# A new fixed order for the first quarter, and a later place for part of the second layer's weight preparation, in a one-core attention and two-layer feed-forward kernel

## The chip, the cores and the metric

One core of a Trainium2 chip. The metric is device time in microseconds (us), the median of several runs. Engines: TensorE (PE in the profile), its weight loads (PEld), VectorE (DVE), ScalarE (ACT), GpSimd (POOL) and SyncE (SP), which issues the DMAs here. Each engine executes its own instructions in the order in which they were put, and waits at each for what it needs of the others.

## What is computed

```python
def _attn_ref(x, state):                      # x (4, 8, 512, 64), state (4, 8, 32, 64)
    scores = scale * np.matmul(x, state.transpose(0, 1, 3, 2))
    a = np.exp(scores - scores.max(-1, keepdims=True))
    a /= a.sum(-1, keepdims=True) + 1e-09
    xread = np.matmul(a, state)
    scores2 = scale * np.matmul(state, x.transpose(0, 1, 3, 2))
    a2 = np.exp(scores2 - scores2.max(-1, keepdims=True))
    a2 /= a2.sum(-1, keepdims=True) + 1e-09
    sread = np.matmul(a2, x)
    return np.concatenate([xread, sread], axis=2)

def _moe_ref(x, w_in, w_out, alpha):          # 2304 tokens, 512 wide, 2048 hidden
    h = x @ w_in
    g = np.maximum(h, 0.0) + alpha * np.minimum(h, 0.0)
    return g @ w_out

def _moe2_ref(x, w_in, w_out):
    h = x @ w_in
    g = np.maximum(h, 0.0) + np.log1p(np.exp(-np.abs(h)))
    return g @ w_out
```

The attention's result, 2304 rows of 512, goes through the first feed-forward layer and that one's result through the second. All of it is float32.

## The kernel before, in words

**Layer 1.** The 2304 rows are four blocks of 512 (the x of one batch entry each) and one of 128 leftover rows (the state rows of all). The hidden width of 2048 is taken in four quarters of 512 (q = 0 to 3), and a quarter's block in four steps of 128 hidden columns: `hidden` makes the product into a bank of the pool `psa` (tiles pa), `act` applies the activation, `out_part` multiplies by the quarter's rows of w_out into banks of `psb` (tiles pb), and `out_take` (L450 on DVE) adds the result to the accumulators acc. Products are made of a high and a low part (names with h and l, L178 to L180: three matmuls of 128x512 each); ACT makes the high part by a rounding copy (L183), the low part is a subtraction (L184).

**Weights.** The 64 weight tiles are loaded by SP into four staging buffers stg (L243) and converted: two ACT steps (L261 exp<-stg, L262 top<-exp), three DVE steps (L266, L272, L276) and one POOL addition (L282). `tick` does one such conversion within a stage, and `conv_head` puts the two ACT steps of the next one ahead. Tiles of layer 2 go back to memory (`kept_w`) until they are used.

**The order.** The first quarter (q = 0), with the attention, is an order written out by hand: the list `ORDER` (L48), whose words are a letter, the step, and a number, its item. `steps` defines a function for each letter: L loads a weight tile, a, j, f, v, g are the conversion steps, x and y load the attention's inputs, s, S, k, t, m, u, e, z, r, n, b, c, d are the row softmax of a half block, M, E, Z, T, K, R, F, X, W the state softmax and read, w, p, q the weight folded with the state, H, A, C, G, D a hidden step with its activation (H on PE, A and G on ACT, C and D on DVE), O its output product, Q its result, and N(i) puts i matmuls of the identity with itself on PE (L640), which nobody reads: fillers. All engines take the list's sequence.

Everything behind the list (quarters 1 to 3 and layer 2) is written in plain loops, and a scheduler puts each engine's order together from it; `tc.issue_after(x)` keeps what is emitted inside from standing ahead of instruction x on its engine.

**The leftover rows** of quarters 1 to 3: `rows_copy` (L385) makes their hidden product (L368 on PE) and copies it by ACT into tmp (L388); `turned_rows` (L391) runs an output product in between and then transposes that copy on PE (L396).

**Layer 2** works on pairs of blocks with seven products of quarter matrices in place of eight (`product`, L585). Its weights come back as raw tiles (`raw_load`, into at0h, at0l, at1h, at1l), and `w_steps(h)` makes from them, for half h of a quarter's columns, the parts nat (wi4, wi5, ex1, wi0) and sums (wi1, ex0, wi2, wi3): eight splits of 128x256, the high parts by ACT (L183), the low parts by POOL (L184), and POOL sums (L488) of 128x128 and 128x256 in between. The steps of half 0 of the first quarter are run by the last quarter of layer 1 (`W_AHEAD`). The steps of half 1 are emitted in the first turn of layer 2 (`p, n` = 0, 0) by `run(w_now, 4)` and `run(w_now)`. The accumulators of the first pair of blocks are prepared by `y_first`: sums on POOL and 14 splits, the last of them of t4 (at7, sw7).

Of the kernel before, what the change touches and what calls it, by code (L numbers as in the profile page):

```python
# [48 lines left out]
N8 N12 L0 a0 U0 x0 s0 P0 L1 N6 k0 x1 j0 f0 v0 t0 s1 a1 M0 g0 L2 x2 y0 L3 m0 j1 e0 E0 L4 a2 z0 Z0 k1 f1 r0 N13 N25 T0  # L49
v1 j2 n0 t1 b0 f2 N29 g1 m1 v2 u1 x3 S2 a3 K0 B0 e1 N3 j3 R0 z1 k3 f3 r1 v3 V0 n1 g2 k2 F0 t3 g3 b1 t2 w00 m2 m3 c0 a4  # L50
X0 W0 e2 p00 j4 z2 w01 f4 u3 r2 c1 p01 H0 N4 q01 L5 H1 A0 e3 v4 n2 a5 C0 g4 b2 z3 L6 j5 r3 G0 A1 N2 H2 c2 C1 a6 f5 d0
H3 x5 x4 L7 w03 G1 D0 j6 D1 h4 l4 n3 L8 A2 f6 C2 p03 v6 g6 A3 h6 d2 d1 O0 v5 b3 c3 G2 g5 q03 a8 w02 M1 d3 p02 D2 C3
q02 G3 h5 D3 M2 a7 j7 f7 v7 H4 A4 l6 l5 S4 k4 H5 E1 x6 E2 L9 A5 O1 j8 C4 f8 y2 g7 C5 v8 a9 L10 O2 t4 k5 h7 l7 g8 T1 T2
H6 O3 H7 G4 G5 A6 D4 j9 t5 y1 M4 D5 f9 m4 u4 m5 v9 C6 E4 Q3 e4 z4 M5 O4 u5 A7 K1 r4 e5 C7 z5 r5 Z2 Z1 n4 n5 G6 O5 K2
a10 R2 D6 b4 G7 M3 R1 F2 c4 E5 F1 T4 X2 O6 Z5 b5 d4 W2 c5 K4 E3 y3 d5 H8 X1 W1 A8 T3 Z3 D7 Z4 j10 C8 f10 K3 y4 L11 x7
H9 A9 C9 R3 F3 O7 S6 G8 G9 Q7 k7 X3 v10 H10 T5 D8 D9 k6 t7 t6 A10 m6 m7 u7 M6 u6 K5 e7 O8 W3 g10 e6 E6 z7 r7 y5 L12
C10 M7 z6 H11 r6 G10 R5 g9 D10 n7 R4 b7 n6 b6 F5 O9 A11 a11 c6 c7 L13 y6 y7 C11 d6 G11 F4 X5 D11 T6 E7 L14 W5 O10 X4
W4 Z7 d7 j11 f11 v11 H12 K6 a12 A12 H13 R6 C12 T7 g11 a13 G12 A13 K7 Z6 j12 O11 f12 C13 H14 D12 H15 v12 j13 g12 F6 G13
Q11 A14 O12 f13 C14 a14 X6 G14 D13 j14 R7 h12 W6 v13 w11 L15 l12 D14 f14 F7 v14 g13 L16 a15 X7 j15 W7 A15 f15 O13 C15
h13 G15 I0 J0 O14 w10 p11 D15 H16 q11 v15 l13 g14 h14 L17 l14 A16 O15 C16 g15 p10 G16 q10 D16 H17 Q15 O16 H18 h15 A17  # L60
A18 H19 H20 C17 G17 C18 G18 A19 Q16 A20 D17 D18 w13 C20 C19 G19 p13 G20 O17 q13 D19 w12 p12 D20 L18 q12 l15
# [22 lines left out]
def mixer_kernel(  # L84
# [199 lines left out]
    acted = {}  # L284
# [100 lines left out]
    def rows_copy(m, q):  # L385
        ps = hidden_rows(m, q)
        hs = tslot()
        nc.scalar.activation(hs, ps, AF.Copy)  # L388
        return hs
# [553 lines left out]
    for q in range(1, NQ):  # L943
# [3 lines left out]
        for b in blocks:  # L947
            for fc in range(4 if b < B else 1):
                if n in TICKS[q]:
                    conv_head()  # L950
# [141 lines left out]
```

## Time and profile before

| | us |
|---|---|
| Median of 3 runs | 712.98 |
| Lowest and highest run | 712.31, 713.21 |
| The profiled execution's own time | 714.09 |
| Its span | 712.2 |
| PE busy, and its share | 700.0 (98%) |
| DVE, ACT, POOL busy | 509.3, 468.1, 358.4 |

The span runs from the first instruction to the last of the profiled execution, and its own time is what that execution took as a whole. A busy PE is not a PE at its peak: the ends of matmuls are modelled, and the fillers count as busy. Windows of the span show which stage a hole belongs to.

### The profile page before, as it was taken

To read this page: it belongs to the slowest core of one execution; us is meant where nothing else is said; L and a number is where in the kernel's file an instruction comes from. 1 tells how busy PE (TensorE), PEld (TensorE's weight loads), DVE (VectorE), ACT (ScalarE), POOL (GpSimd) and SP (SyncE) were. 2 spreads that over 40 slices of the span, in tenths; PEclk is the share of its full clock that TensorE was granted. 3 is DMA by queue.
4 is the path that set the end of the run, shared out by engine and by line. 5 is a ranking of instruction groups with operands and counts; after the bars stand their busy time and mean duration, and the time that the engine had idled before them with its cause. 6 is when DMAs were issued, how large, how long until landed. Compare 5 with 4: busy or idle time off the path is not lost.

```text
span 712.2 us, 10216 instructions
## 1 busy us (share of the span) xinstructions
PE 700.0 (98%) x3530; PEld 548.0 (77%) x3530; DVE 509.3 (72%) x832; ACT 468.1 (66%) x921; POOL 358.4 (50%) x401
## 2 busy tenths in 40 slices
PE   8999999999999999989999999999999999999997
PEld 6457776677777777858888888888888888888886
DVE  4897786479999989788455577747675546677665
ACT  4777796556665656556569777557885877676541
POOL 2463223023334323597975594096998666454110
PEclk9999999999999999999999999999999999999999
DMA  8352532131552365545300522002205221210003
GB/s 296 106 170 84 192 115 91 30 118 58 178 164 93 131 210 173 193 149 169 120 8 1 177 75 104 20 26 88 60 2 177 75 89 30 89 30 30 2 29 119
DMA packets 30484, 72.49 MB, mean 102 GB/s; under 512 B 3552, under 2 KB 3552, under 8 KB 30432
## 3 DMA queue, kind: packets, MB, share of 16 engines
q1 hardware_dynamic: 30432, 71.83, 31.0%
q8 instruction: 28, 0.46, 0.3%
q14 instruction: 24, 0.20, 0.1%
HBM read 58.97 MB, written 12.85 MB: 101 GB/s over the span
## 4 chain that ended last, share of the span: by engine, by line
PE 87%; DVE 4%; DMA 3%; ACT 3%; POOL 1%; issue 1%; SPq 1%; POOLq 0%; ACTq 0%
PE pa L585 21%; PE pb L178 16%; PE pb L179 16%; PE pb L180 16%; PE pa L178 4%; PE pa L180 4%; PE pa L179 4%; PE pa L332 2%; DMA acc<-xt 2%; PE pa L368 1%; DVE stg L276 1%; DMA stg<-w1o 1%; DMA stg<-w1i 1%; PE pa L396 0%; POOL stg L282 0%
## 5 line engine op out<-in xcount | busy, mean ns | idle before, releaser
L282 POOL TENSOR_TENSOR stg<-top,stg 128x512 f32<-128x512 bf16 x48 | 58.4, 1217 | 105.0 <-DVE stg L276 79.5
L607 DVE TENSOR_TENSOR acc<-pb,acc 128x512 f32<-128x512 f32 x112 | 74.5, 686 | 25.0 <-PE pb L180 24.1
L404 DVE SCALAR_TENSOR_TENSOR pa<-tmp,rest,pa 128x512 f32<-128x512 f32 (+1 forms) x80 | 52.8, 668 | 24.2 <-ACT tmp L412 15.3
L415 ACT ACTIVATE tmp<-pa 128x512 f32<-128x512 f32 x68 | 40.2, 594 | 40.5 <-DVE pa L488 27.1
L418 DVE SCALAR_TENSOR_TENSOR pa<-pa,tmp 128x512 f32<-128x512 f32 x68 | 46.8, 694 | 14.4 <-ACT tmp L417 14.0
L266 DVE SCALAR_TENSOR_TENSOR top<-stg,top 128x512 uint16<-128x512 uint16 x63 | 50.8, 809 | 7.8 <-ACT top L262 7.7
L261 ACT ACTIVATE exp<-stg 128x512 bf16<-128x512 bf16 x63 | 41.9, 667 | 19.0 <-DMA stg<-w2i 5.3
L262 ACT ACTIVATE top<-exp,top_bias 128x512 uint16<-128x512 uint16 x64 | 46.1, 722 | 12.6 <-POOL stg L282 6.9
L416 ACT ACTIVATE tmp<-tmp 128x512 f32<-128x512 f32 x68 | 42.3, 630 | 0.7
L417 ACT ACTIVATE tmp<-tmp 128x512 f32<-128x512 f32 x68 | 42.3, 629 | 0.6
L488 DVE TENSOR_TENSOR pa<-pa,wo2l 128x512 f32<-128x512 f32 x32 | 22.2, 696 | 27.3 <-PE pa L585 27.3
L276 DVE SCALAR_TENSOR_TENSOR stg<-stg,exp 128x512 f32<-128x512 uint32 x48 | 40.7, 850 | 1.0
L450 DVE TENSOR_TENSOR acc<-pb,acc 128x512 f32<-128x512 f32 x54 | 35.1, 684 | 4.3 <-PE pb L180 4.3
L412 ACT ACTIVATE tmp<-pa 128x512 f32<-128x512 f32 x47 | 27.4, 590 | 12.4 <-PE pa L180 7.2
L488 DVE TENSOR_TENSOR wo2h<-pa,wo2h 128x512 f32<-128x512 f32 x16 | 11.1, 691 | 27.5 <-ACT wo2h L1000 15.6
L183 ACT ACTIVATE g1h<-pa 128x512 fp32r<-128x512 f32 x26 | 15.5, 596 | 17.3 <-DVE pa L404 9.2
L272 DVE TENSOR_SCALAR exp<-top 128x512 uint16<-128x512 uint16 x64 | 26.1, 409 | 0.9
L184 POOL TENSOR_TENSOR ex1l<-at1h,ex1h 128x256 fp32r<-128x256 f32 x16 | 11.8, 739 | 26.9 <-ACT ex1h L183 24.6
L184 POOL TENSOR_TENSOR wi4l<-at0h,wi4h 128x256 fp32r<-128x256 f32 x16 | 11.9, 743 | 23.1 <-ACT wi4h L183 23.1
L488 DVE TENSOR_TENSOR wo2l<-pa,wo2h 128x512 f32<-128x512 f32 x16 | 11.0, 690 | 15.8 <-PE pa L585 15.8
L184 DVE TENSOR_TENSOR g3l<-pa,g3h 128x512 fp32r<-128x512 f32 x22 | 15.2, 690 | 9.5 <-ACT g3h L183 9.4
L183 ACT ACTIVATE g0h<-pa 128x512 fp32r<-128x512 f32 x23 | 13.8, 598 | 12.4 <-DVE pa L404 10.2
(808 smaller groups left out, 2459.9 us busy)
## 6 DMA issues: line engine op xcount, KB each, us to landing
stg<-w1o SPq DMA_DIRECT2D x16, 511.8 KB, 3.9
stg<-w2i SPq DMA_DIRECT2D x16, 511.8 KB, 4.3
stg<-w2o SPq DMA_DIRECT2D x16, 511.8 KB, 3.5
stg<-w1i SPq DMA_DIRECT2D x15, 511.8 KB, 4.7
acc<-xt SPq DMA_DIRECT2D x16, 256.0 KB, 5.5
wi<-stg SPq DMA_DIRECT2D x16, 256.0 KB, 3.1
wo<-stg SPq DMA_DIRECT2D x16, 256.0 KB, 2.9
out<-acc SPq DMA_DIRECT2D x16, 256.0 KB, 3.0
```

Source lines behind the costliest of these rows:

```text
L178: nc.tensor.matmul(ps, lh, rh, start=start, stop=False)
L179: nc.tensor.matmul(ps, lh, rl, start=False, stop=False)
L180: nc.tensor.matmul(ps, ll, rh, start=False, stop=stop)
L262: nc.scalar.activation(t.bitcast(U16), e.bitcast(U16), AF.Relu, bias=top_bias, scale=TOP_SCALE)
L266: nc.vector.scalar_tensor_tensor(out=tu, in0=words(i)[0], scalar=TOP_SIGN, in1=tu, op0=ALU.bitwise_and, op1=ALU.bitwise_or)
L276: nc.vector.scalar_tensor_tensor(out=a, in0=words(i)[1], scalar=REST, in1=parts(i)[1], op0=ALU.mult, op1=ALU.mult)
L282: nc.gpsimd.tensor_tensor(out=a, in0=parts(i)[0], in1=a, op=ALU.add)
L404: nc.vector.scalar_tensor_tensor(out=ps[:, cs], in0=t[:, cs], scalar=a, in1=ps[:, cs], op0=ALU.mult, op1=ALU.add)
L418: nc.vector.scalar_tensor_tensor(out=ps, in0=ps, scalar=0.0, in1=t, op0=ALU.max, op1=ALU.add)
L488: eng.tensor_tensor(out=o, in0=x, in1=y, op=op)
L585: nc.tensor.matmul(ps, l[:, c], r, start=first and k == 0 and i == 0, stop=k == 1 and i == 2, skip_group_check=not first,)
L607: nc.vector.tensor_tensor(out=a, in0=ps, in1=a, op=ALU.add)
```

## The change

It has three parts.

1. The list `ORDER` is another one: the same steps and items except for the fillers, in another sequence. Of each the first line, and two lines around the second block's first steps:

```diff
-N8 N12 L0 a0 U0 x0 s0 P0 L1 N6 k0 x1 j0 f0 v0 t0 s1 a1 M0 g0 L2 x2 y0 L3 m0 j1 e0 E0 L4 a2 z0 Z0 k1 f1 r0 N13 N25 T0
...
-q02 G3 h5 D3 M2 a7 j7 f7 v7 H4 A4 l6 l5 S4 k4 H5 E1 x6 E2 L9 A5 O1 j8 C4 f8 y2 g7 C5 v8 a9 L10 O2 t4 k5 h7 l7 g8 T1 T2
-H6 O3 H7 G4 G5 A6 D4 j9 t5 y1 M4 D5 f9 m4 u4 m5 v9 C6 E4 Q3 e4 z4 M5 O4 u5 A7 K1 r4 e5 C7 z5 r5 Z2 Z1 n4 n5 G6 O5 K2
...
+L0 N1 N6 N5 N12 P0 U0 x0 s0 a0 N3 L1 j0 L2 k0 a1 x1 f0 v0 N3 t0 M0 m0 N4 g0 y0 L3 e0 N3 s1 j1 z0 r0 E0 n0 k1 N2 T0 N11
...
+h5 p02 q02 d1 M2 x4 h6 a8 a7 j7 f7 M1 H5 l5 v7 S4 H4 E2 A4 j8 L9 A5 C5 C4 f8 y1 v8 O1 k4 M4 t4 E1 l6 g7 G4 k5 h7 l7 H6
+D4 O2 G5 g8 y2 H7 L10 A6 a9 T2 T1 O3 D5 C6 j9 E4 m4 t5 m5 u5 f9 M5 v9 u4 a10 A7 Q3 e4 O4 z4 e5 r4 C7 z5 E5 K1 K2 O5 G6
```

The fillers (N) are 102 before and 84 now.

2. The leftover rows' product and copy are emitted ahead of `conv_head`, no longer behind it. 3. In the first turn of layer 2, `run(w_now, 4)` stands under `tc.issue_after(first_act)`, where `first_act` is the last rounding copy (L183) that `act` gave ACT in layer 1.

```diff
@@ -946,9 +947,10 @@
         n = 4 if second else 0
         for b in blocks:
             for fc in range(4 if b < B else 1):
+                hs = rows_copy(0, q) if b == B else None
                 if n in TICKS[q]:
                     conv_head()
-                ps = hidden(0, q, b, fc) if b < B else turned_rows(rows_copy(0, q), lambda: out_part(*todo.pop(0)))
+                ps = hidden(0, q, b, fc) if b < B else turned_rows(hs, lambda: out_part(*todo.pop(0)))
                 g = act(0, q, b, fc, ps)
                 if len(todo) >= LAG:
                     out_part(*todo.pop(0))
@@ -985,6 +987,7 @@
             pair_out(*before[:2], j, before[2][j])
         act_all()
 
+    first_act = acted["ACT"]
     for p in range(2):
         for n in range(8):
             q, h = divmod(n, 2)
@@ -1017,7 +1020,8 @@
             act_all((a, q, gs[0], 0), (d, q, gs[1], 1))
             if (p, n) == (0, 7):
                 run(y_now, 4)
-            run(w_now, 4)
+            with tc.issue_after(first_act) if start else nullcontext():
+                run(w_now, 4)
             if (p, n) == (0, 6):
                 y_now = y_second()
                 run(y_now, 4)
```

What this moves, by the order of instructions on the engines (lines of the changed kernel are one higher up to L949):

ACT in the head, the first score blocks. L742 (L743) is the exponential of a half block, acc_104 that of the third; L850 (L851) are the four small copies of the first state read, sw0h and sw1h the first folded weights. Before:

```order
L836 ACTIVATE acc_107<-pa_411,stn_85 128x128
L782 ACTIVATE at0h<-wo4h 128x512
L261 ACTIVATE exp_74<-stg_67 128x512
L262 ACTIVATE top_72<-exp_74,top_bias 128x512
L850 ACTIVATE srh<-pa_411 64x32 x4
L742 ACTIVATE acc_104<-acc_104 128x512
L861 ACTIVATE sw0h<-pa_447 128x512
L861 ACTIVATE sw1h<-pa_448 128x512
```

Now:

```order
L263 ACTIVATE top_72<-exp_74,top_bias 128x512
L743 ACTIVATE acc_104<-acc_104 128x512
L862 ACTIVATE sw0h<-pa_430 128x512
L862 ACTIVATE sw1h<-pa_431 128x512
L783 ACTIVATE at0h<-wo4h 128x512
L743 ACTIVATE acc_100<-acc_100 128x512
L862 ACTIVATE sw2h<-pa_440 128x512
L862 ACTIVATE sw3h<-pa_441 128x512
L262 ACTIVATE exp_75<-stg_64 128x512
L263 ACTIVATE top_73<-exp_75,top_bias 128x512
L898 ACTIVATE tmp_69<-pa_470 128x512
L851 ACTIVATE srh<-pa_388 64x32 x4
```

The four small copies stood ahead of the exponential of acc_104, and now stand behind the first tmp.

ACT somewhat later, up to g0h of the second block. exp and top rows are conversions, L897 (L898) is the first activation step of a hidden product, L906 (L907) its rounding copy, L800 (L801) a state softmax. Before:

```order
L261 ACTIVATE exp_75<-stg_66 128x512
L262 ACTIVATE top_73<-exp_75,top_bias 128x512
L897 ACTIVATE tmp_70<-pa_657 128x512
L713 ACTIVATE wi5l<-pa_667 128x512
L800 ACTIVATE ex1h,stn_86<-ex1h,stn_86 128x512
L800 ACTIVATE ex1l,stn_87<-ex1l,stn_87 128x512
L897 ACTIVATE tmp_71<-pa_678 128x512
L261 ACTIVATE exp_75<-stg_64 128x512
L262 ACTIVATE top_73<-exp_75,top_bias 128x512
L713 ACTIVATE srl<-pa_668 128x512
L682 ACTIVATE wo3h<-stg_66 128x512
L906 ACTIVATE g0h<-pa_657 128x512
```

Now:

```order
L862 ACTIVATE sw5h<-pa_604 128x512
L683 ACTIVATE wo2h<-stg_65 128x512
L262 ACTIVATE exp_74<-stg_67 128x512
L263 ACTIVATE top_72<-exp_74,top_bias 128x512
L262 ACTIVATE exp_75<-stg_66 128x512
L263 ACTIVATE top_73<-exp_75,top_bias 128x512
L801 ACTIVATE ex1l,stn_87<-ex1l,stn_87 128x512
L898 ACTIVATE tmp_70<-pa_657 128x512
L898 ACTIVATE tmp_71<-pa_638 128x512
L714 ACTIVATE wi5l<-pa_647 128x512
L801 ACTIVATE ex1h,stn_86<-ex1h,stn_86 128x512
L907 ACTIVATE g0h<-pa_657 128x512
```

Before, the conversion of stg_64 (a load of w1i) stands ahead of g0h; now those of stg_67 and stg_66 stand together ahead of tmp_70 and tmp_71, and that of stg_64 comes five rows behind g0h.

POOL in the last quarter of layer 1. L282 (L283) is a conversion's addition, the L184 rows (L185) of 128x256 are splits of layer 2's first weights, the L488 rows (L489) their sums. Before:

```order
L184 TENSOR_TENSOR wi4l<-at0h,wi4h 128x256
L282 TENSOR_TENSOR stg_67<-top_72,stg_67 128x512
L488 TENSOR_TENSOR at0h<-at0h,at1h 128x128
L184 TENSOR_TENSOR wi5l<-at0l,wi5h 128x256
L184 TENSOR_TENSOR ex1l<-at1h,ex1h 128x256
L184 TENSOR_TENSOR wi0l<-at1l,wi0h 128x256
L488 TENSOR_TENSOR at0h<-at0h 128x128
L282 TENSOR_TENSOR stg_64<-top_73,stg_64 128x512
L184 TENSOR_TENSOR wi4l<-at0h,wi4h 128x256
L488 TENSOR_TENSOR at0l<-at0l,at1l 128x128
L488 TENSOR_TENSOR at1h<-at1h,at0h 128x256
L282 TENSOR_TENSOR stg_65<-top_72,stg_65 128x512
```

Now:

```order
L283 TENSOR_TENSOR stg_67<-top_72,stg_67 128x512
L283 TENSOR_TENSOR stg_64<-top_73,stg_64 128x512
L185 TENSOR_TENSOR wi4l<-at0h,wi4h 128x256
L489 TENSOR_TENSOR at0h<-at0h,at1h 128x128
L489 TENSOR_TENSOR at0h<-at0h 128x128
L283 TENSOR_TENSOR stg_65<-top_72,stg_65 128x512
L185 TENSOR_TENSOR wi5l<-at0l,wi5h 128x256
L489 TENSOR_TENSOR at0l<-at0l,at1l 128x128
L489 TENSOR_TENSOR at0l<-at0l 128x128
L283 TENSOR_TENSOR stg_66<-top_73,stg_66 128x512
L185 TENSOR_TENSOR ex1l<-at1h,ex1h 128x256
L489 TENSOR_TENSOR at1h<-at1h,at0h 128x256
```

Before, wi4l of half 1 follows that of half 0 two conversions later, and sums of both halves stand mixed; now only half 0 stands here, and the first four splits of half 1 come behind the split of sw4, ahead of that of at7, in layer 2's first turn.

## Rows read from the trace of the kernel before

**Rows 1.** Windows: us, busy us by engine (instructions), clock, DMA share, GB/s.

```profile
0.00:60.00 60.00, 55.06 (x353) 33.96 (x354) 46.06 (x82) 39.86 (x76) 26.83 (x27) 1.00 0.55 189
...
296.00:320.00 24.00, 20.82 (x86) 15.35 (x85) 18.64 (x25) 15.21 (x32) 23.90 (x30) 1.00 0.46 152
320.00:712.00 392.00, 388.31 (x1722) 320.97 (x1720) 248.44 (x395) 260.88 (x518) 234.62 (x286) 1.00 0.21 69
...
344.00:368.00 24.00, 24.00 (x108) 19.88 (x107) 11.08 (x18) 13.94 (x25) 21.36 (x18) 1.00 0.12 36
```

**Rows 2.** PE's waits from 0 to 60 us: us in total, times, longest.

```profile
PE pa L332 <- DVE sw6l L867: 1.1, 1, 1.1
...
PE pa L178 <- DVE g0l L911: 0.7, 1, 0.7
```

**Rows 3.** DVE's waits from 10 to 57 us.

```profile
DVE g0l L911 <- ACT g0h L906: 2.1, 1, 2.1
DVE sts L746 <- ACT acc L742: 1.7, 1, 1.7
```

**Rows 4.** Groups by shape, POOL, 296 to 320 us: busy us, mean ns.

```profile
L184 POOL TENSOR_TENSOR wi4l<-at0h,wi4h 128x256 fp32r<-128x256 f32 x2 | 1.5, 740 | 3.0 <-ACT wi4h L183 3.0
...
L488 POOL TENSOR_TENSOR at1h<-at1h,at0h 128x256 f32<-128x256 f32 x2 | 1.5, 731 | 0.0
...
L488 POOL TENSOR_TENSOR at0h<-at0h 128x128 f32<-128x128 f32 x2 | 1.0, 486 | 0.0
```

**Rows 5.** Timeline 305.5 to 309.5 us: start, us, line [idle <-releaser].

```profile
305.92 0.72 ACT L262 ACTIVATE top<-exp,top_bias 128x512 uint16<-128x512 uint16 x1 [0.36 <-POOL stg L282]
...
307.95 0.68 DVE L450 TENSOR_TENSOR acc<-pb,acc 128x512 f32<-128x512 f32 x1
...
308.78 0.47 PE L178 MATMUL pb<-g3h,wo5h 128*128 128x512 f32 x1 [1.58 <-DVE acc L450]
```

**Rows 6.** Timeline 313 to 317 us, PE at the transposes of the leftover rows.

```profile
316.09 0.66 PE L396 MATMUL pa<-ident,tmp 128*128 128x128 f32 x4 [1.61 <-ACT tmp L388]
```

**Rows 7.** Timeline 357 to 368 us, the last split of t4 and its use.

```profile
360.71 1.30 POOL L184 TENSOR_TENSOR sw7l<-acc,sw7h 128x512 fp32r<-128x512 f32 x1
...
366.98 0.39 PE L585 MATMUL pa<-sw7l,wi0h 128*128 128x512 f32 x1
```

**Rows 8.** Timeline 33 to 36 us, a small DVE step beside a POOL split.

```profile
33.45 1.79 POOL L788 TENSOR_TENSOR at0l<-wo4h,at0h 128x512 fp32r<-128x512 f32 x1
...
34.03 1.25 DVE L751 TENSOR_SCALAR sts<-sts 128x16 f32<-128x16 f32 x1
```

**Rows 9.** Timeline 21 to 22 us, DVE.

```profile
21.23 0.28 DVE L272 TENSOR_SCALAR exp<-top 128x512 uint16<-128x512 uint16 x1
21.43 0.17 DVE L751 TENSOR_SCALAR sts<-sts 128x16 f32<-128x16 f32 x1
```

**Rows 10.** Groups by shape, DVE, 10 to 57 us.

```profile
L266 DVE SCALAR_TENSOR_TENSOR top<-stg,top 128x512 uint16<-128x512 uint16 x8 | 6.5, 808 | 0.3 <-ACT top L262 0.3
...
L276 DVE SCALAR_TENSOR_TENSOR stg<-stg,exp 128x512 f32<-128x512 uint32 x4 | 3.5, 885 | 0.0
L272 DVE TENSOR_SCALAR exp<-top 128x512 uint16<-128x512 uint16 x8 | 3.5, 433 | 0.0
...
L751 DVE TENSOR_SCALAR sts<-sts 128x16 f32<-128x16 f32 x4 | 1.8, 438 | 0.0
...
L266 DVE SCALAR_TENSOR_TENSOR top<-acc,top 128x512 uint16<-128x512 uint16 x1 | 0.7, 680 | 0.0
```

**Rows 11.** Timeline 24 to 31 us, ACT, the small copies.

```profile
26.98 0.56 ACT L850 ACTIVATE srh<-pa 64x32 f32<-64x32 f32 x4 [1.77 <-PE pa L840]
```

**Rows 12.** Chain that ended last, 45 to 57 us: start, us, what.

```profile
48.61 4.38 DMA stg<-w1i
```

**Rows 13.** Timeline 1 to 18 us, PE, two runs of fillers.

```profile
1.36 4.53 PE L640 MATMUL pb<-ident 128*128 128x128 f32 x20 [1.36 <-POOL ident masks.py:199]
...
12.12 4.37 PE L640 MATMUL pb<-ident 128*128 128x128 f32 x38
```

## What the change should do to the time

> **What bounds the kernel now.** The profiled execution took 714.09 us, of which 712.2 us is the span; the median of the three runs is 712.98 us, so the profiled one lies 1.11 us above it. I work out a difference and set it against the median. I read stages first, then what TensorE (PE) waited for in those with holes, then the engines behind the waits.
>
> By stage [rows 1], PE is busy for 388.31 of the last 392 us, and the few that lack are the end of the program; 108 matmuls take 24.00 us there, 0.22 us each. Such a stage gives nothing back unless matmuls go away, and only fillers do. Two stages have holes: the first 60 us (55.06 busy, part of it fillers) and 296 to 320 us (20.82 of 24). The change can be worth something there alone, and it touches both.
>
> In the head PE waited 1.1 us for VectorE's (DVE's) sw6l and 0.7 us for its g0l [rows 2]; DVE itself waited 2.1 and 1.7 us on ScalarE (ACT) [rows 3]. At 296 to 320 us the reader sees two PE waits: 1.58 us for an accumulation bank that DVE had not emptied [rows 5], 1.61 us for ACT's copy of the leftover rows [rows 6].
>
> I take 0.2% (1.4 us) as what a measurement of this kernel can tell from no change.
>
> **The second half of the first weights (issue_after).** In the old order of POOL the splits and sums of both halves stand in the last quarter of layer 1 among the weight conversions; in the new one the second half stands behind the last activation. POOL is the queue that this relieves: 23.90 of 24 us busy [rows 1]. A split costs it 0.74 us, a small sum 0.49, a wide one 0.73 [rows 4]. What leaves is four splits, four small and two wide sums: 3.0 + 2.0 + 1.5 = 6.4 of the 23.9 us (the half's other four splits come later still). The chain of the first stall can be read off [rows 5]: ACT's conversion step at 305.92 was released by POOL's L282, and the L450 that empties PE's bank stands in DVE's queue behind that conversion's next steps, at 307.95; PE came 1.58 us late. The second is the same backlog a tick later: the copy L388 stands behind a conversion step in both orders, and that step had been held up as before. With 6.4 us less on POOL the conversions come earlier by more than 1.6 us, so I take both stalls away. Of 3.2 us I count **3.0**, since a hand-over of a tenth or two stays; ends 0 and 3.2.
>
> What the moved work meets: it lands in the turn, where POOL is busy 21.36 of 24 us [rows 1]. Its four splits (3.0 us) stand before at7l, wo5l, sw7l and wo6l. In the old order sw7l ended at 362.0 and PE used it at 366.98 [rows 7]; 3.0 us later it ends at 365.0, with 2.0 us to spare, and the turn as a whole moves with PE. ACT gets four splits ahead of at7h, with 13.94 of 24 us busy there [rows 1]. So I price this at **nothing**; from 2 us on, every further microsecond that POOL comes later is PE's.
>
> **The leftover rows' copy, written ahead of the conversion.** In two of the three quarters its row in ACT's queue is where it was; in the second quarter (q = 1) it now stands behind one conversion step more, 0.72 us at most [rows 5]. PE has other work between those rows and their transposes, from 308.78 to 316.09 us less the wait in the case shown [rows 5, 6], so **nothing**; without that cover 0.72 us.
>
> **The list of the first quarter.** Up to the second g0l (block 1) DVE has the same instructions in both orders and one reduction more in the new one, which it then has behind it. PE, in the new order, does H6 and H7 before the transposed tiles that need g0l's bank, where the old one came to H6 and stood; with more work ahead of that point a wait for g0l is less likely. What DVE wastes before it in the old order is 2.1 + 1.7 us of waits [rows 3] and stretched steps. A 128x16 step took 1.25 us with POOL's split beside it [rows 8], 0.17 without [rows 9]. By groups, against a step that stands alone: L266 8 x (0.81 - 0.68), L276 4 x (0.89 - 0.68), L272 8 x (0.43 - 0.28), L751 4 x (0.44 - 0.17) [rows 9, 10], that is 1.0 + 0.8 + 1.2 + 1.1 = 4.1 us.
>
> - The 1.7 us goes: DVE waited for ACT's L742, behind four small copies (L850) that had waited 1.77 us for PE [rows 11]. In the new order L742 comes before them.
> - The 2.1 us goes in its old form: g0h stood behind a conversion whose load was issued at 48.61 and took 4.38 us [rows 12]. In the new order that conversion comes after g0h.
> - But two conversion pairs, 4 x 0.72 us at most [rows 5], now stand on ACT between sw5h and the next activations, while DVE has little more than the rest of sw4l and sw5l and one reduction to do: an idle of about 2.1 us, an estimate from these. Between the first two activations stand the four small copies (0.56 us [rows 11]), one copy and a pair, some 2.5 us against about 1.6 us of DVE's steps: 0.9 us, an estimate too.
> - Of the 4.1 us of stretching the bounds are nothing and all. The same POOL instructions run beside it in both orders, and only their order can part them; I take a third, **1.4**, nearer the lower end, because old and new order differ by a few places for most of these steps.
>
> Sum: 1.7 + 2.1 + 1.4 - 2.1 - 0.9 = **2.2 us**; ends 0.8 and 4.9, and below nothing if such new idles come once more. PE can use it: the long stages have hardly a hole [rows 1], so a head that ends 2.2 us sooner moves all that follows. The list's fillers fall from 102 to 84; they fill holes, so their number costs nothing by itself.
>
> The Trainium skill has a rule for the stretching (page "SBUF — State Buffer", section "Who interferes with whom"): VectorE and GpSimd share one port pair, held for a whole instruction, which VectorE takes for two SBUF inputs or in a two-port mode. The trace agrees on L751, 1.25 us in place of 0.17. By that rule alone an order without overlaps would save the whole 4.1 us, and the forecast would be 2.7 us lower.
>
> **Sum.** 3.0 + 2.2 = 5.2 us: **707.8** against the median, 708.9 for an execution like the profiled one.
>
> **Rivals.**
> - *Only the stage gains.* The head's new idles eat what it saves. For it: the pairs need a place on ACT, wherever they are put. 712.98 - 3.0 = 710.0.
> - *Only the head gains.* The stalls stay, as the first half's work and the conversions still fill POOL. Against it: 6.4 of 23.9 us leave. 710.8.
> - *The turn gives it back.* POOL comes 4 us or more beyond the 2.0 us to spare, and PE waits before sw7l or the second half's sums: 707.8 + 4 = about 712.
> - *The clock.* The first 20 fillers took 4.53 us, 0.23 each, 38 later ones 4.37 us, 0.12 each [rows 13], so the array ran at the lower of its levels at first; the granted clock reads 1.00 in every stage [rows 1], which is 2.4 GHz. Should a hole of the new head bring it down to 1.2 GHz for as long as at the start, some 9 us (the first fillers lie before 10 us, the quick ones behind 12), 4.5 us are lost: 712.3. Against it: no stage shows a fall. The Trainium skill says that such a fall follows an idle PE (page "TensorE: Matmul & The Clock Gate", section "HAM oscillation — how this bites in real kernels"); no row here shows one.
> - *Slower.* ACT reaches the two conversion pairs before their loads. It runs in order, so the activations, g0h and the DVE steps behind them stand still. The load of rows 12 landed at 53.0; if one of the pair's does so, with ACT there at about 44, 9 us are lost: 707.8 + 9 = 716.8. It makes the kernel slower from a standstill of 6.6 us (5.2 + 1.4). Against it: the new order issues one of these loads earlier than the old.
> - *Nothing in sum.* The head loses about what the stage gains: 713.
>
> **Chances.** Forecast 0.54, only the stage 0.16, only the head 0.10: faster 0.80. The turn 0.05, the clock 0.04, nothing in sum 0.04: same 0.13. The late load: slower 0.07. The range reaches down to both full ends, 712.98 - 3.2 - 4.9 = 704.9, and up over the single gains, the turn and the clock to 712.3; the slower case, nothing in sum and the tails of the others are left out.
>
> **What would show it.** Right: PE busy 23.5 us or more of the 24 in which the leftover rows of the last quarter stand, no PE wait there for the L450 and L388 of now (their lines one further), gaps in POOL's queue; DVE at the second g0l some 2 us sooner, its waits of 1.7 and 2.1 us gone; no PE wait in the turn. Wrong: a PE wait for sw7l or the second half's sums; ACT's conversion steps released by loads between 40 and 50 us; a granted clock under 1.00 after the first 15 us; PE's block 1 ending no sooner than now.

## The result, and the profile after

| | before | after |
|---|---|---|
| Median, us | 712.95 (4 runs) | 706.17 (4 runs, 704.83 to 706.60) |
| Ratio to before, 95% interval | | 0.9897 (0.9885 to 0.9910) |
| The profiled execution, and its span | 714.09, 712.2 | 705.88, 704.1 |

The change saves 6.8 us by the medians, where 5.2 was forecast. The two profiled executions differ by 8.2 us: the one of before lies 1.1 us above its median, and the table of starts below shows that this sits in its first 40 us. I therefore read each part from several executions, not from this pair alone. Line numbers are one higher than before up to L949.

The stages of after, as windows; the columns are us, then PE, PEld, DVE, ACT and POOL busy (instructions), clock, DMA share, GB/s. The second is the stretch that was 296 to 320 us before, the last the turn that was 344 to 368 [rows 1].

```profile
0.00:60.00 60.00, 56.18 (x356) 35.67 (x357) 48.10 (x89) 44.39 (x85) 27.23 (x28) 1.00 0.51 180
288.00:312.00 24.00, 22.32 (x94) 16.91 (x93) 21.84 (x33) 13.81 (x25) 14.73 (x16) 1.00 0.58 191
312.00:704.00 392.00, 388.36 (x1723) 321.00 (x1721) 247.16 (x391) 263.09 (x526) 242.39 (x298) 1.00 0.21 69
336.00:360.00 24.00, 24.00 (x108) 19.87 (x107) 11.07 (x18) 14.56 (x28) 24.00 (x24) 1.00 0.09 23
```

In the last quarter of layer 1 POOL is busy for 14.73 us in place of 23.90, and PE for 22.32 in place of 20.82: one of the two stalls is gone, and one is left. The timeline there, ACT and then PE:

```profile
306.99 0.67 ACT L262 ACTIVATE exp<-stg 128x512 bf16<-128x512 bf16 x1 [1.09 <-DMA stg<-w2o]
307.55 0.58 ACT L389 ACTIVATE tmp<-pa 128x512 f32<-128x512 f32 x1
...
308.19 0.66 PE L397 MATMUL pa<-ident,tmp 128*128 128x128 f32 x4 [1.68 <-ACT tmp L389]
```

The chain of waits of after names that load:

```profile
302.97 3.93 DMA stg<-w2o
```

The leftover rows' copy (L389) still stands behind a conversion step, and that step stands still until its weight tile has landed at 306.90. Before, the same step had waited for DVE:

```profile
314.88 0.67 ACT L261 ACTIVATE exp<-stg 128x512 bf16<-128x512 bf16 x1 [0.44 <-DVE stg L276]
```

The turn itself is dense: POOL is full there, and no wait of PE falls in it. The last split of t4 and its use [rows 7 are before's]:

```profile
355.04 1.35 POOL L185 TENSOR_TENSOR sw7l<-acc,sw7h 128x512 fp32r<-128x512 f32 x1
...
359.05 0.39 PE L586 MATMUL pa<-sw7l,wi0h 128*128 128x512 f32 x1
```

It ends 2.66 us before PE needs it; before, 4.97 us.

In the head, DVE's waits from 10 to 53 us:

```profile
DVE stn L796 <- ACT ex0l L714: 1.9, 1, 1.9
DVE top L267 <- ACT top L263: 1.8, 1, 1.8
...
DVE sw2l L868 <- ACT sw2h L862: 0.2, 1, 0.2
```

The waits of 1.7 and 2.1 us [rows 3] are gone, and one of 1.8 us has come. The wait at the top, for ex0l, is old: 1.5 us before. DVE's groups by shape in the same stretch (busy us, mean ns), against [rows 10]:

```profile
L267 DVE SCALAR_TENSOR_TENSOR top<-stg,top 128x512 uint16<-128x512 uint16 x7 | 6.2, 887 | 1.8 <-ACT top L263 1.8
...
L277 DVE SCALAR_TENSOR_TENSOR stg<-stg,exp 128x512 f32<-128x512 uint32 x4 | 2.6, 667 | 0.0
L273 DVE TENSOR_SCALAR exp<-top 128x512 uint16<-128x512 uint16 x8 | 2.5, 319 | 0.0
...
L277 DVE SCALAR_TENSOR_TENSOR wi0l<-stg,exp 128x512 f32<-128x512 uint32 x1 | 0.8, 819 | 0.0
...
L752 DVE TENSOR_SCALAR sts<-sts 128x16 f32<-128x16 f32 x4 | 0.7, 166 | 0.0
```

By the prediction's own measure (7 x 0.21 for L267, 8 x 0.04 for L273, one L277 of 0.82 in place of 0.68) 1.9 of the 4.1 us of stretching is left: 2.2 us are saved. From the first g0l to the second, as a window over DVE, before and then after:

```profile
36.25:56.09 19.84, 17.34 (x29) 1.00 0.61 196
```

```profile
34.98:52.30 17.32, 15.09 (x27) 1.00 0.63 211
```

Its idle time there hardly changes (2.50 and 2.23 us). Its busy time does, by 2.25 us. About 0.6 of this is work that stands elsewhere: between the two g0l the old order has a step L266 and the split of at2l, the new one has these ahead of the first g0l and one reduction in their place. The other 1.6 us is stretching: added up over the conversion steps of this window, what they take beyond their time alone is 1.7 us before and 0.1 after.

Starts of PE's milestones, read from the timelines of eight executions: the first and second block's first output product (pb<-g0h,wo0h), the leftover rows' transposes of the second and third quarter, the first product of layer 2. The kernels other than before and after are the experiments below.

| start, us | 1st block | 2nd block | rows q=1 | rows q=2 | layer 2 |
|---|---|---|---|---|---|
| before (old list) | 39.21 | 62.42 | 158.83 | 235.55 | 347.03 |
| later_alone (old list) | 37.60 | 60.99 | 157.46 | 234.18 | 342.99 |
| fewer_fillers (old list) | 37.53 | 60.73 | 157.15 | 233.87 | 345.79 |
| after (new list) | 37.33 | 57.62 | 152.46 | 229.41 | 339.10 |
| list_alone (new list) | 38.13 | 58.32 | 153.16 | 230.11 | 342.08 |
| rows_first (new list) | 38.24 | 58.47 | 153.37 | 230.31 | 338.13 |
| two_moves (old list, edited) | 38.31 | 60.65 | 157.11 | 233.83 | 345.75 |
| pool_twice (new list) | 37.56 | 62.32 | 157.31 | 234.26 | 342.43 |

Two things are to be seen. Up to the first block, executions of one list differ by up to 1.7 us among themselves, and the lists by 0.2 on the mean (38.1 and 37.9), which is less than that spread. From there on, pieces repeat in the first six rows: first to second block 23.2 to 23.4 us with the old list and 20.2 to 20.3 with the new one; second block to the rows of q=1 96.4 to 96.5 and 94.8 to 94.9. The list's gain is made behind the first block, in two pieces of 3.0 and 1.6 us. Of the second, 0.2 us is only one 128x512 matmul that stands ahead of those rows in the old order and behind them in the new: from the rows of q=1 to those of q=2 the old list takes 76.7 us and the new one 76.9. That leaves 3.0 and 1.3 us.

The first piece can be read off PE's rows. The work from block to block is the same number of matmuls of each kind. Before:

```profile
41.84 0.39 PE L180 MATMUL pb<-g0h,wo0l 128*128 128x512 f32 x1
43.37 1.04 PE L332 MATMUL pa<-wi0h,ex0h 64*32 64x512 f32 x2 [1.14 <-DVE sw6l L867]
...
45.16 0.50 PE L178 MATMUL pa<-at2h,sw2h 128*128 128x512 f32 x1
...
55.49 0.60 PE L632 MATMUL pa<-ident,ex1l 128*128 128x128 f32 x4
56.83 0.50 PE L178 MATMUL pa<-at2h,sw2h 128*128 128x512 f32 x1 [0.74 <-DVE g0l L911]
```

And after, where neither wait is:

```profile
39.98 0.39 PE L181 MATMUL pb<-g0h,wo0l 128*128 128x512 f32 x1
40.29 0.61 PE L333 MATMUL pa<-wi0h,ex0h 64*32 64x512 f32 x1
...
41.42 0.50 PE L179 MATMUL pa<-at2h,sw2h 128*128 128x512 f32 x1
...
54.44 0.60 PE L633 MATMUL pa<-ident,ex1h 128*128 128x128 f32 x4
54.80 0.48 PE L179 MATMUL pb<-g3h,wo3h 128*128 128x512 f32 x1
```

From the block's last output matmul to the next 128x512 product PE takes 3.32 us before and 1.44 after; from the last transposes to what follows them, 1.34 and 0.36. Together 2.9 of the 3.0 us sit at these two waits, which are listed with 1.9 (1.14 and 0.74); the rest is the slower start behind each.

### The profile page after: what moved, and what is told of

Its sections match the earlier page's. It is cut to its first block, busy times and chain, and to the rows that moved or that the text cites. A ratio compares the mean times of both kernels' runs of the same rounds, so it can differ in the third digit from the quotient of the medians.

```text
span 704.1 us, 10175 instructions
## 1 busy us (share of the span) xinstructions
PE 694.9 (99%) x3512; PEld 545.6 (77%) x3512; DVE 506.3 (72%) x832; ACT 468.7 (67%) x921; POOL 355.0 (50%) x401
## 4 chain that ended last, share of the span: by engine, by line
PE 92%; DMA 3%; DVE 1%; POOL 1%; ACT 1%; issue 1%; SPq 0%; POOLq 0%; ACTq 0%
PE pa L586 22%; PE pb L179 17%; PE pb L181 17%; PE pb L180 17%; PE pa L179 4%; PE pa L181 4%; PE pa L180 4%; PE pa L333 2%; PE pa L369 1%; DMA stg<-w2o 1%; DMA acc<-xt 1%; DMA wo4l<-wo 1%; PE pa L633 1%; PE pb L641 1%; PE pb L700 1%
## 5 line engine op out<-in xcount | busy, mean ns | idle before, releaser
L283 POOL TENSOR_TENSOR stg<-top,stg 128x512 f32<-128x512 bf16 x48 | 58.4, 1218 | 102.7 <-DVE stg L277 74.6
L405 DVE SCALAR_TENSOR_TENSOR pa<-tmp,rest,pa 128x512 f32<-128x512 f32 (+1 forms) x80 | 53.0, 670 | 27.3 <-ACT tmp L413 14.8
L267 DVE SCALAR_TENSOR_TENSOR top<-stg,top 128x512 uint16<-128x512 uint16 x63 | 51.3, 816 | 8.1 <-ACT top L263 8.0
L489 DVE TENSOR_TENSOR pa<-pa,wo2l 128x512 f32<-128x512 f32 x32 | 22.2, 695 | 25.4 <-PE pa L586 25.3
L277 DVE SCALAR_TENSOR_TENSOR stg<-stg,exp 128x512 f32<-128x512 uint32 x48 | 38.8, 810 | 1.0
L451 DVE TENSOR_TENSOR acc<-pb,acc 128x512 f32<-128x512 f32 x54 | 35.1, 683 | 4.3 <-PE pb L181 4.3
L489 DVE TENSOR_TENSOR wo2h<-pa,wo2h 128x512 f32<-128x512 f32 x16 | 11.0, 690 | 27.9 <-ACT wo2h L1003 18.1
L185 POOL TENSOR_TENSOR ex1l<-at1h,ex1h 128x256 fp32r<-128x256 f32 x16 | 11.9, 746 | 32.6 <-ACT ex1h L184 26.3
L184 ACT ACTIVATE g1h<-pa 128x512 fp32r<-128x512 f32 x26 | 15.5, 596 | 19.3 <-DVE pa L405 10.9
L273 DVE TENSOR_SCALAR exp<-top 128x512 uint16<-128x512 uint16 x64 | 24.4, 381 | 1.0
L184 ACT ACTIVATE g0h<-pa 128x512 fp32r<-128x512 f32 x23 | 13.7, 595 | 13.8 <-DVE pa L405 11.7
L185 POOL TENSOR_TENSOR wo5l<-wo5l,wo5h 128x512 fp32r<-128x512 f32 x8 | 10.4, 1299 | 22.1 <-ACT wo5h L184 19.7
L489 DVE TENSOR_TENSOR wo2l<-pa,wo2h 128x512 f32<-128x512 f32 x16 | 11.0, 690 | 14.2 <-PE pa L586 14.1
L185 DVE TENSOR_TENSOR g2l<-pa,g2h 128x512 fp32r<-128x512 f32 x24 | 16.5, 687 | 6.5 <-ACT g2h L184 6.2
```

Source lines behind the costliest of these rows:

```text
L267: nc.vector.scalar_tensor_tensor(out=tu, in0=words(i)[0], scalar=TOP_SIGN, in1=tu, op0=ALU.bitwise_and, op1=ALU.bitwise_or)
L283: nc.gpsimd.tensor_tensor(out=a, in0=parts(i)[0], in1=a, op=ALU.add)
L405: nc.vector.scalar_tensor_tensor(out=ps[:, cs], in0=t[:, cs], scalar=a, in1=ps[:, cs], op0=ALU.mult, op1=ALU.add)
L489: eng.tensor_tensor(out=o, in0=x, in1=y, op=op)
```

## The experiments

**The two parts by themselves.** list_alone is before with the new `ORDER`; later_alone is before with

```diff
+    first_act = acted["ACT"]
...
-            run(w_now, 4)
+            with tc.issue_after(first_act) if start else nullcontext():
+                run(w_now, 4)
```

Of list_alone was expected:

> The kernel before with the new list alone. The recorded prediction gives the list 2.2 us: about 710.8. The traces of before and after put more there: the first matmul of the second block's output starts 4.8 us sooner (62.42 and 57.62 us), the leftover rows of the second quarter 6.4 us sooner (158.83 and 152.46 us), in two executions whose own difference is 8.2 us where the medians differ by 6.8. By that reading the list carries about 5 us: 707 to 708.5, and this run has both of before's PE waits of 296 to 320 us (for an L450 and an L388, 1.6 us each). A rival by which the list only matters together with the later place of the weight steps gives 711.5 or more.

It took 708.60 us, ratio 0.9935 (0.9920 to 0.9950). Of later_alone:

> The kernel before with the later place of half 1's first steps alone. The recorded prediction takes both PE waits of the last quarter away: 3.0 us, 710.0. The trace of after shows only one of the two gone (the wait for L450) and the wait for the leftover rows' copy still there with 1.66 us, now behind a conversion step that waits for its load: by that 1.5 to 1.8 us, about 711.3, with a PE wait of 1.3 to 2.0 us for L388. A rival by which the turn of layer 2 gives it back: a new PE wait behind 344 us, and 712.5 or more.

It took 710.30 us, ratio 0.9956 (0.9944 to 0.9969). Its PE waits from 290 to 400 us, the whole list:

```profile
PE pa L396 <- ACT tmp L388: 0.8, 1, 0.8
```

So the list is worth 4.3 us (712.91 - 708.60) and the later place 2.6 (712.91 - 710.30), together 6.9 where both at once gave 6.8: the parts add up, and neither needs the other. The list is nearly double what the prediction gave it, and came out just above the 707 to 708.5 us expected; the later place is worth less than its 3.0 us, and lies between the 710.0 of the prediction and the 711.3 of the expectation. As expected from after's trace, the wait for L450 goes and that for L388 does not; the latter is shorter in this trace than expected (0.8 us, and 1.7 in after). From the third quarter's rows to layer 2 the trace shows 111.5 us before and 108.8 here.

The remaining part, the rows' copy ahead of `conv_head`, has no run of its own. list_alone is without it and after has it: in their traces ACT, DVE and POOL have the same instructions in the same order up to 288 us, where the later place begins to show, and in all three quarters the copy stands right behind the same conversion step.

**The stall that is left.** rows_first is after with the conversion held behind the copy:

```diff
-        nc.scalar.activation(hs, ps, AF.Copy)
+        i = nc.scalar.activation(hs, ps, AF.Copy)
+        if m == 0:
+            acted["ACT"] = i.ins
         return hs
```

(`conv_head` issues its two ACT steps behind `acted["ACT"]`.)

> The kernel after with one thing more: a conversion's two ACT steps may not stand ahead of the leftover rows' copy, in all three quarters. If the wait of 1.66 us is only the copy's place behind a conversion step that waits for a load, it goes: 1.4 to 1.7 us less than after, about 704.6, and no PE wait for L389 in the last quarter. If the load then holds up the next activation instead (the tmp that stands behind the conversion), PE waits a little later for a bank or for that activation and less than 0.5 us is gained. In the other two quarters PE had no such wait, so nothing changes there.

It took 705.00 us, ratio 0.9883 (0.9867 to 0.9900), 1.2 us below after, a little less than expected; the two intervals overlap, so what settles the matter is the trace. The window over the same stage, and the timeline of ACT in it:

```profile
289.00:313.00 24.00, 24.00 (x103) 18.53 (x102) 22.03 (x33) 15.12 (x29) 15.46 (x18) 1.00 0.60 192
```

```profile
305.17 0.59 ACT L389 ACTIVATE tmp<-pa 128x512 f32<-128x512 f32 x1
306.38 0.66 ACT L262 ACTIVATE exp<-stg 128x512 bf16<-128x512 bf16 x1 [0.62 <-DMA stg<-w2o]
```

The copy now runs before the load has landed, the conversion still waits for it, and the trace lists no PE wait from 60 to 700 us. That settles the second stall: it was the copy's place behind a step that waits for a load, and not POOL's backlog.

**What in the list gains: single waits?** two_moves takes the old list and removes by hand the two waits that the prediction's sum began with:

```diff
-X0 W0 e2 p00 j4
+X0 e2 p00 W0 j4
...
-... v8 a9 L10 O2 ...
-H6 O3 H7 G4 G5 A6 D4 j9
+... v8 L10 O2 ...
+H6 O3 H7 G4 G5 a9 A6 D4 j9
```

> The kernel before with the old list and two of its items moved by hand: the four small copies of the first state read behind the exponential and the first folded weights, and one conversion's ACT steps behind the second block's first two rounding copies. If VectorE's two waits (1.7 and 2.1 us) are what the new list takes away, nearly all of the list's gain comes with them: 3 us or more, 710 or less. If they are only a part, as PE's own waits for sw6l and g0l (1.1 and 0.7 us) bound what it sees of them, and VectorE meets a new idle of about 1 us at the moved conversion's next step, 0.8 to 2 us: 711 to 712.2. A rival by which the moved items only wait elsewhere: no difference, 713.

It took 712.31 us, ratio 0.9986 (0.9975 to 0.9998): 0.6 us by the medians. That figure is soft, since its twelve executions lie in two groups: five took 710.74 to 711.01 us and seven 712.30 to 713.81. Five of the seven have a mean granted clock of 0.996 or 0.997, all others 0.999 or 1.000. By the lower group alone the two moves would be worth about 2 us, half of what the list gives. The trace is that of an execution of 712.76 us. DVE's window between the two g0l, and the wait that has come in an earlier place:

```profile
35.36:53.20 17.84, 17.42 (x28) 1.00 0.56 175
```

```profile
29.38 0.69 DVE L867 TENSOR_TENSOR sw2l<-pa,sw2h 128x512 fp32r<-128x512 f32 x1 [1.22 <-ACT sw2h L861]
```

The 2.1 us is truly gone (0.42 us idle in place of 2.50), so the second g0l comes 2.0 us sooner behind the first, but busy time stays at 17.4. PE had only waited 0.7 us for that g0l, and its path from block to block shortens by 0.9 (22.34 in place of 23.2). Of the 1.7 us, 1.0 came back in the wait shown (1.22, of which 0.25 was there before). PE's wait for sw6l stays (1.3 us). three_moves takes that one too:

```diff
-... v6 g6 A3 h6 d2 d1 O0 v5 b3 c3 G2 g5 q03 a8 w02 ...
+... v6 g6 A3 q03 h6 d2 d1 O0 v5 b3 c3 G2 g5 a8 w02 ...
```

> The kernel with two items of the old list moved, and a third: the low parts of the fourth pair of folded weights (sw6l, sw7l) stand on VectorE ahead of three steps (at2l, a conversion's last step, a transpose) that stood ahead of them. In the old list's executions sw6l comes 6.4 us behind the first g0l, with the new list 3.3 us behind it, and PE waits 1.1 to 1.3 us for it with the old one alone. If the place of sw6l is a main part of what the new list gains, PE's wait for it is gone and the time falls by 1 to 1.9 us against two_moves: 710.4 to 711.3. If only the wait for g0l counted, or if PE meets the three later steps next (at2l above all, for the hidden product that reads it), it stays within 0.4 us of 712.3.

It took 712.15 us, ratio 0.9996 (0.9986 to 1.0006), and missed what the first theory asked for. Eight of its twelve executions took 711.85 to 712.28 us, the other four 713.35 to 715.53; the trace is that of one of the four (713.62). PE's waits from 30 to 60 us in it:

```profile
PE pa L178 <- DVE g2l L911: 1.8, 1, 1.8
PE pb L178 <- DVE at2l L788: 0.8, 1, 0.8
```

The wait for sw6l is gone and 2.6 us of others stand in its place: in this execution what is moved ahead on DVE pushes something else behind. An execution near the median may have had less of it; none was traced. Three of the old list's waits, taken away by hand, give 0.6 us by the medians; the relisted whole gives 4.3.

**What in the list gains: steps beside POOL?** pool_twice is after with each of POOL's splits in the list done twice (the same values again):

```diff
-            nc.gpsimd.tensor_tensor(out=lo, in0=rounded[i], in1=hi, op=ALU.subtract)
+            for _ in range(2):
+                nc.gpsimd.tensor_tensor(out=lo, in0=rounded[i], in1=hi, op=ALU.subtract)
...
-            eng.tensor_tensor(out=lo, in0=live["b", i], in1=hi, op=ALU.subtract)
+            for _ in range(2 if eng is nc.gpsimd else 1):
+                eng.tensor_tensor(out=lo, in0=live["b", i], in1=hi, op=ALU.subtract)
```

> The kernel after with each of POOL's splits in the list (L689 and L791 here) done twice, so that POOL writes the same low part again: seven more steps of 1.3 us ahead of the second block's output. It measures what a POOL step beside VectorE costs it. If VectorE's word steps (L266, L272, L276, L751 of the kernel before) stretch beside POOL, its busy time from the first to the second g0l rises from 15.2 us by 0.7 to 3 us, by these steps alone and not by those that read an accumulation bank (L405, L868, L912), and the end comes 0.5 to 2.5 us later: 706.7 to 708.7. If the stretching in the trace of before was something else, the busy time stays within 0.3 us of 15.2, and the end moves only as far as POOL's own later steps (sums, additions of conversions) make VectorE or ACT wait.

It took 709.46 us, ratio 0.9955 (0.9943 to 0.9968), 3.3 us above after (on another chip, where before took 712.54 us). DVE's window between the two g0l, and four of its steps in it:

```profile
35.22:56.63 21.41, 19.19 (x27) 1.00 0.48 160
```

```profile
36.61 0.74 DVE L405 SCALAR_TENSOR_TENSOR pa<-tmp,rest,pa 128x512 f32<-128x512 f32 x1
...
38.90 0.68 DVE L870 TENSOR_TENSOR sw6l<-pa,sw6h 128x512 fp32r<-128x512 f32 x1
...
46.75 1.81 DVE L267 SCALAR_TENSOR_TENSOR top<-stg,top 128x512 uint16<-128x512 uint16 x1 [1.76 <-ACT top L263]
48.60 1.24 DVE L273 TENSOR_SCALAR exp<-top 128x512 uint16<-128x512 uint16 x1
```

The same 27 instructions keep DVE busy for 19.19 us in place of 15.09; its idle is unchanged (2.22 us). The steps that stretch are the word steps, as in before: 1.81 against 0.68 alone, 1.24 against 0.28. Those that read an accumulation bank (L405, L870) keep their 0.74 and 0.68 us. Both shown here lie wholly beside a POOL step. It is more than I expected (0.7 to 3 us): 4.1 us, where five of the seven added POOL steps, of 1.3 to 1.6 us each, fall into the window. Part of the 3.3 us at the end is PE waiting for the later splits themselves (1.5 us for wo1l, 0.9 for at3l), so the time of the run is not the price of stretching alone; DVE's busy time is.

**The fillers.** fewer_fillers is before with `N29` made `N11`, no_fillers is after with no N at all.

> The kernel before with 18 of its 102 fillers left out, in its longest run of them (29 made 11), which gives it as many as the new list has. The recorded prediction prices the fillers' number at nothing: no difference, within 0.7 us of 712.9, with PE idle in their place. A rival reads the 1.9 us that the fillers take less in the trace of after as part of the gain: 18 x 0.115 us = 2.1 us less, 710.8.

713.33 us, ratio 1.0007 (0.9998 to 1.0015): their number costs nothing, as the prediction said, and the time that they take less in after's trace (12.9 us in place of 15.2; the expectation's 1.9 is too low) is no part of the gain.

> The kernel after with none of its 84 fillers; PE stands idle in their place. If they only fill holes and nothing hangs on them, no difference: 706.2 within 0.7. If they are what holds TensorE at its upper level in the head, the products of the head run at the lower one for a while (128x512 matmuls 0.43 us apart in place of 0.23): some 40 of these, the scores and the folded weights lie before 45 us, so 2 to 8 us more, 708 to 714, and a granted clock of 0.5 or little more in some windows before 45 us.

707.03 us (704.88 to 707.62), ratio 0.9913 (0.9899 to 0.9927), which overlaps after's interval and lies between the two outcomes expected. The first block's product starts at 39.54 us, 1.3 to 2.2 later than in the new list's other executions, and of this the last quarter's stall gives 0.8 back (0.9 us in place of 1.7: the load lands 1.3 us later than in after, at 308.19, and PE's other work there comes 2.1 us later). The same four transposes without fillers, and with them in after:

```profile
14.85 1.11 PE L633 MATMUL pa<-ident,ex0l 128*128 128x128 f32 x4 [0.74 <-ACT ex0l L801]
```

```profile
13.59 0.66 PE L633 MATMUL pa<-ident,ex0l 128*128 128x128 f32 x4
```

Without fillers the array is still at the slower of its rates at 15 to 17 us; at 23.47 us the next four take 0.66 too. What fillers buy is that, 1 to 2 us of head, and the end hardly sees it while the stall for the load remains.

**Two tries at more.** x1_early is rows_first with the second half block's x loaded ahead of two weight tiles; x0_early is that, with the state and first x ahead of the first weight tile too:

```diff
-L0 N1 N6 N5 N12 P0 U0 x0 s0 a0 N3 L1 j0 L2 k0 a1 x1 f0
+L0 N1 N6 N5 N12 P0 U0 x0 s0 a0 N3 x1 L1 j0 L2 k0 a1 f0
...
-L0 N1 N6 N5 N12 P0 U0 x0 s0 a0 N3 x1 L1
+U0 x0 L0 P0 N1 N6 N5 N12 s0 a0 N3 x1 L1
```

> The kernel rows_first with one thing more: the first list loads the second half block's x (two tiles, which land at 11.5 us in the trace of after, and for which PE waits 0.9 to 2.1 us) ahead of two weight tiles. If that load bounds the head, the first g0l comes 0.5 to 1.5 us sooner and so does the end: 703.5 to 704.5. If the conversions of the two weight tiles, now later, bound it (the folded weights need them at 24 us), no gain or up to 1 us of loss: 705 to 706.

704.20 us (703.81 to 704.53), ratio 0.9878 (0.9864 to 0.9892): the lowest of all, by 0.8 us against rows_first, though the two intervals overlap. The step from after to rows_first is the part of it that a trace settles.

> The kernel x1_early with one thing more: the state and the first half block's x are loaded ahead of the first weight tile. In the trace of x1_early the chain of the first 36 us begins with that x (issued at 2.12 us, landed at 6.9), and SP needs 0.4 to 0.5 us per load, so it should land 0.5 to 1 us sooner and the end come as much sooner: 703.2 to 703.8. The first conversion starts later for it, by about as much as the x comes sooner or more; if VectorE's steps up to the first folded weights hang on it, no gain or a loss: 704.2 to 705.5.

705.30 us, ratio 0.9896 (0.9881 to 0.9911), on the other chip: 1.1 us above x1_early, with intervals that overlap. If it is a loss, its trace offers two reasons. DVE's first wait:

```profile
DVE top L267 <- ACT top L263: 9.4, 1, 9.4
```

It begins its first conversion only after a wait of 9.4 us (5.9 in x1_early), since the first weight tile lands at 8.81 us in place of 5.30. ACT's copy of the first scores (L716) stands behind that conversion, PE waits for it, and then the granted clock, third from the end, falls:

```profile
10.78 0.66 PE L635 MATMUL pb<-ident,ex0l 128*128 128x128 f32 x4 [2.29 <-ACT ex0l L716]
```

```profile
12.00:14.00 2.00, 2.00 (x12) 0.44 (x10) 1.97 (x5) 0.95 (x3) 1.16 (x1) 0.50 1.05 408
```

The eight matmuls of the next scores (L702) take 1.93 us there, and 1.06 in x1_early. The first g0l comes at 36.39 us in place of 35.35. How much of this is the later conversion and how much the clock was not separated.

## Why the prediction was right in sum, and where it was wrong

The time, the range and the sign held. Both terms were off, the one too high and the other too low, so the sum is better than its parts, and that is luck.

*The bound.* Right for layer 2, which takes 365.2 us before and 365.0 after from its first product on. Wrong in "The change can be worth something there alone": 1.3 us of the list's gain lie between the second block and the rows of q=2, behind the 60 us named, where PE is busy nearly throughout, before and after:

```profile
60.00:160.00 100.00, 99.86 (x696) 73.94 (x695) 71.48 (x129) 68.03 (x151) 26.31 (x22) 1.00 0.32 101
```

```profile
57.62:152.46 94.84, 94.84 (x677) 70.54 (x675) 69.60 (x126) 65.35 (x146) 24.47 (x21) 1.00 0.34 111
```

The busy time holds pauses of about 0.1 to 0.4 us between kinds of matmul, and so a full stage can still give something back to another order.

*The second half's later place, 3.0 us forecast; 2.6 alone, 2.4 on top of the list (708.60 - 706.17).* The failed sentence is "The second is the same backlog a tick later ... so I take both stalls away". The first stall went as described, with POOL relieved by more than was forecast (from 23.90 to 14.73 us, 9.2 in place of 6.4). The second did not: the step ahead of the copy waits for a load, which rows_first shows by moving the copy. In the trace of before that step waited for DVE, and I did not ask what it would wait for once DVE and POOL come sooner. PE's listed waits of the stage and the turn, 3.4 us before (1.6, 1.6 and 0.2), are 1.7 in after and 0.8 in later_alone: 1.7 to 2.6 us by the traces.

*Priced at nothing in the turn.* Right. sw7l came 2.3 us later against its use, and 2.66 us were left.

*The leftover rows' copy.* Right, and for a simpler reason than the cover: it moves nothing. The conversion step that now stands ahead of it in the second quarter comes with the new list.

*The list, 2.2 us forecast; 4.3 measured.* DVE's side of the sum was close. Over three executions each, the second g0l comes at 55.04 us with the old list (56.09, 54.67, 54.37) and at 52.90 with the new (52.30, 53.11, 53.30): 2.1 us. Inside it the sizes were off and cancelled in part: stretching gave 2.2 in place of 1.4 (the third taken was a choice between the bounds); the wait of 2.1 us is replaced by one of 1.8, as estimated; the new idle of 0.9 us did not appear (0.2); and the gain of 1.7 us is not to be seen at the first block, where both lists stand at the same time. The step that failed is the one from DVE to PE: "a head that ends 2.2 us sooner moves all that follows" took the second g0l for the head's end. PE's second block starts 3.2 us sooner (61.4 and 58.1 on the mean of the three), since the wait for sw6l [rows 2] goes as well, and H6 and H7 now cover the second g0l: 2.9 us by the rows shown above. Another 1.3 us follows behind the second block, where the trace lists no PE wait in either kernel: the same matmuls but one stand there in another order, with fewer and shorter pauses between kinds of matmul (up to the rows of q=1 the products of folded weights, L332, take 4.96 us before and 4.24 after, single transposes 0.94 and 0.51, from start to start; the leftover rows' product, L368, goes the other way, 6.06 and 6.55). Which of the moved items does that was not tried, nor whether the weight loads take part, some of which wait for ACT or DVE there, up to 0.9 us each, in both traces.

*The rule of the Trainium skill* (page "SBUF — State Buffer", section "Who interferes with whom"): by it a step of POOL and a step of VectorE that reads two inputs from SBUF or runs in a two-port mode do not run side by side. pool_twice agrees: L267, whose two inputs lie there, and the small L273 stretch; L405 and L870, which read one of their two from an accumulation bank, do not. The price can also fall on POOL: in the same trace a split of at0l that starts at 30.07 us, just behind an L267 of 30.03, takes 1.79 us in place of 1.27, and that L267 its usual 0.69. As a forecast of this list, an order without overlaps was too much: 1.9 of the 4.1 us are still there.

*The rivals.* "Only the stage" and "only the head" are excluded by the two single runs. The turn gave nothing back. The late loads did not stop ACT: it had no wait for a load from 36 to 53 us. The clock did not fall in the traces of before and after. It did in two others: in the last quarter in list_alone (below), and in x0_early in the head, where the prediction had looked for it, but for less than half of the 9 us that it assumed.

*What would show it.* Of the signs named, POOL's gaps, the waits of 1.7 and 2.1 us gone, the second g0l and the silent turn came. PE's 23.5 us in the rows' stage did not (22.32), and it was the sign that told the term wrong.

## What to carry to other kernels

When a wait is to be removed, list everything that the waiting instruction and the one ahead of it in its queue need, and ask which is next to end: here POOL, then a load. On a saturated engine, a wait that is taken away can come back as others; what helped here was the order as a whole. Busy time that shrinks by more than the instructions that left is a sign of two engines that exclude each other, so count the instructions of both windows first. Price a change of a head at the engine that bounds what follows, not at the engine that was studied, and take milestones from several executions before splitting a gain among parts. Where a kernel's executions lie in two groups, say which of them the trace is from.

## What was not expected of the hardware

The granted clock can fall behind a single stall some 300 us into the program. In list_alone's profile PE waited 2.11 us in the last quarter (for L451); its rows, and the windows of that stretch, with the granted clock third from the end:

```profile
303.87 0.47 PE L179 MATMUL pb<-g3h,wo5h 128*128 128x512 f32 x1 [2.11 <-DVE acc L451]
...
305.57 0.63 PE L179 MATMUL pb<-g3h,wo5h 128*128 128x512 f32 x1
306.00 0.63 PE L180 MATMUL pb<-g3l,wo5h 128*128 128x512 f32 x1
...
308.73 0.39 PE L180 MATMUL pb<-g3l,wo5h 128*128 128x512 f32 x1
```

```profile
302.00:304.00 2.00, 0.13 (x1) 0.16 (x2) 1.97 (x4) 0.42 (x1) 2.00 (x4) 1.00 0.89 256
304.00:306.00 2.00, 2.00 (x8) 1.55 (x9) 2.00 (x4) 1.58 (x4) 2.00 (x4) 0.75 0.28 107
306.00:308.00 2.00, 2.00 (x6) 1.62 (x5) 2.00 (x4) 1.30 (x3) 2.00 (x4) 0.50 0.81 211
```

The matmuls from 303.87 to 304.86 start 0.23 to 0.31 us apart, those from 305.14 to 308.13 about 0.43: the clock is granted at half, 1.2 GHz, and comes back. That run lost little by it, since the copy's stall shrank from 1.6 to 0.2 us. Stalls of 1.6 to 2.1 us in the profiles of before, two_moves and fewer_fillers show no such fall, so it does not always come. x0_early's fall, from 11.6 to 15.0 us, also came right behind a stall, of 2.29 us. That such falls are part of what a stall costs on the median is possible: the clocks of two_moves' executions point that way, but the one trace of its upper group shows no fall, so it is not shown.

The granted clock of a window does not tell of the start: in no_fillers it reads 1.00 in every window up to 20 us, while four transposes take 1.11 us there and 0.66 later. The trace's clock records explain it: they begin only at 23.02 us in that run (10.48 in before, 5.83 in after), just where PE's matmuls become faster, and a window ahead of them is printed as 1.00. So without fillers PE reached its upper rate 17 us later than in after, and the end came only 0.9 us later.
